# Attention's output written straight into the MLP's layout in 32-row groups, units in pairs, and keys turned by VectorE

## The chip, the cores and the metric

One Trainium2 chip, of which the kernel uses one core. The metric is the device time of one execution in microseconds (us); lower is better. "Time before" is the median of three runs.

## The reference, cut to what matters

```python
def _attn_ref(q, k, v, f_logit):                  # each (4, 8, 768, 48): batch, head, step, feature
    f = 1.0 / (1.0 + np.exp(-f_logit))
    for t in range(S):
        state = f[:, :, t, :, None] * state + np.einsum('bhd,bhe->bhde', k[:, :, t], v[:, :, t])
        y[:, :, t] = np.einsum('bhd,bhde->bhe', q[:, :, t], state)
    return y
x = _attn_ref(...).transpose(0, 2, 1, 3).reshape(3072, 384)
x = np.square(np.maximum(x @ w_in, 0)) @ w_out                         # MLP 1, 384 -> 2048 -> 384
h = x @ w_in2; return (h * np.tanh(softplus(h))) @ w_out2              # MLP 2, the same sizes
```

A recurrent attention with a forget gate for each feature, then two MLPs over the 3072 tokens.

## The kernel before, in words

**The MLPs.** Tokens are taken in 6 blocks of 512, the 2048 hidden features in 16 chunks, so an MLP has 96 *slots*. In a slot TensorE (PE) does `do_l1(i)`: nine 128x512 products into a PSUM tile `h` (L333), and `do_l2(i-2)`: nine into the three accumulators `a` (L344). Nine and not three because operands are split into a high and a low part (weights `w`, x, and gh/gl). Between the two, ScalarE (ACT) does `act_a` (relu, square, the high part gh) and VectorE (DVE) `act_b` (the low part gl, L357). The second MLP works alike with a longer activation; nothing of the change lies there.

**The attention** feeds the first MLP. The 768 steps are 12 chunks of 64, and each chunk is done for two pairs of batches: 24 *units*. Four units (two chunks) make one token block's x. A unit has y = 0 and 1 for the two batches of its pair, and does:

- `load_f`, `load_v` (SyncE's queue): the gates, keys and queries `in`, and the values `vs`;
- `v_min`, `a_exp`, `a_ln`, `v_scan`, `a_dq`, `a_dk`, `v_q`, `v_k` on DVE and ACT: the running product of gates and the scaled queries `mv` (L449) and keys (L453);
- `m_a` on PE: keys times queries (`at` L476/477, or `aq` L471 in four 64x64 quadrants of PE's array from unit 9 on); `v_mask` (L495/L498) masks it into `mv`;
- `m_t` on PE: four transposes of the keys into a PSUM tile `tr` (L486), which `a_kn` copies to `kn` by four ACT instructions (L508);
- `m_u` on PE: keys times values, the update of the state (`u` L543/544, `uq` L538 in quadrants); `v_s` (L588, L589) puts the new state beside the values of unit i+2 in `vs`;
- `m_y` on PE: y = masked products and queries times values and state. For units 0 to 7 (L518) tokens lie on the partitions, two tiles of 64 columns of the array side by side; `a_y` (ACT, L553) copies it, and `m_x` (PE, L577) transposes it into `xt`. For units 8 to 23 (L525) features lie on the partitions, 48 of 64 rows for a head; `a_y` (L558) copies it, and `y_dma` (L565 to L570) moves it by six DMAs into `ax` with the rows in the MLP's order;
- `a_x` (L602), `v_x` (L606): high and low part of x for the MLP.

**PSUM.** `h`, `at`, `aq`, `tr`, `u`, `uq`, `y` and `xt` share five banks of one pool; the accumulators have three.

**Order.** Engines run their instructions in the order of the program. Up to slot 18 this order is a list written by hand (`START`). From there `put(slot, prio, f, ...)` collects the operations of a slot and `run(i)` issues them sorted by prio; `unit(i, s)` puts those of unit i around its slot s = 4i - 17, so one unit every four slots: `m_a`, `m_t` in slot s between `do_l1` (prio 100) and `do_l2` (prio 120), `m_y`, `m_u` in slot s+2. In slots 22 to 70 the second MLP's weights are also prepared (`w2_load`, `w2_abs`, `w2_bits`, `w2_split`: L251 to L261, L306, L307).

**fp32 products in the trace.** The attention's matmuls are plain fp32, and one of them shows as two records of PE. A *round* below is the stretch in which matmuls in different tiles of the array run at once.

Of the kernel before, what the change touches and what calls it, by code (L numbers as in the profile page):

```python
# [42 lines left out]
v_k 3; v_k 2; v_q 3 1; w_low 0; m_x 0; a_x 0; m_u 0; a_kn 1; v_s 0 0; m_a 2; w_abs 1; v_x 0; load_w 3; v_mask 2 0;
m_u 1; v_s 1 0; v_s 0 1; w_shift 1; m_a 3; m_t 3; v_mask 2 1; w_hi 0; a_kn 3; m_t 2; m_warm 1; m_y 2; a_kn 2;
v_s 1 1; v_mask 3 1; v_mask 3 0; m_x 1; m_warm 1; m_y 3; m_warm 1; w_lo 0; w_top 1; load_w 4; w_abs 2; a_x 1; v_x 1;
a_y 2; w_shift 2; m_x 2; load_f 5; a_y 3; w_low 1; a_x 2; load_w 5; m_x 3; m_warm 6; load_w 6; v_end 3; a_x 3; v_x 3;
v_x 2; w_top 2; do_l1 0; w_hi 1; w_abs 3; load_v 4; w_lo 1; w_low 2; do_l1 1; w_abs 4; w_shift 3; v_min 5; w_hi 2;
load_w 7; w_top 3; a_exp 5; w_lo 2; w_shift 4; m_u 3; load_w 8; w_low 3; act_a 0; act_b 0; w_abs 5; w_top 4; w_hi 3;
w_shift 5; load_w 9; do_l1 2; act_a 1; w_lo 3; w_low 4; w_hi 4; act_b 1; load_w 11; w_top 5; w_lo 4; w_low 5;
v_s 3 0; do_l2 0; do_l1 3; do_l2 1; act_a 2; act_b 2; do_l1 4; w_abs 6; w_hi 5; w_abs 7; w_shift 6; w_lo 5; w_top 6;  # L50
do_l2 2; act_a 3; w_abs 8; w_shift 7; w_low 6; load_f 4; a_ln 5; w_hi 6; w_top 7; act_b 3; v_s 3 1; act_a 4; w_lo 6;
w_abs 9; do_l1 5; do_l2 3; w_low 7; w_hi 7; load_v 5; act_b 4; w_shift 8; load_f 7; act_a 5; w_shift 9; load_w 10;
do_l1 6; w_top 8; load_f 6; do_l2 4; v_end 2; w_lo 7; w_top 9; w_low 8; act_b 5; act_a 6; w_hi 8; w_abs 11; v_min 4;
v_scan 5; w_lo 8; load_v 7; do_l1 7; w_low 9; load_w 14; a_exp 4; do_l2 5; a_ln 4; act_b 6; a_dq 5; w_hi 9; a_dk 5;
v_q 5 1; w_abs 10; w_lo 9; v_scan 4; do_l1 8; act_a 7; do_l2 6; v_k 5; a_dq 4; v_q 5 0; act_a 8; do_l1 9; a_dk 4;
w_shift 10; act_b 7; w_top 10; v_q 4 1; m_t 5; v_min 6; w_shift 11; v_k 4; act_a 9; act_b 8; m_a 5; load_w 12;
do_l2 7; v_min 7; m_u 2; v_q 4 0; do_l2 8; w_low 10; a_kn 5; m_a 4; w_top 11; m_t 4; a_exp 7; v_mask 5 0; w_hi 10;
a_ln 7; w_lo 10; v_end 5; v_end 4; w_low 11; act_b 9; w_abs 12; w_hi 11; w_shift 12; v_mask 5 1; w_top 12; do_l1 10;
do_l2 9; w_lo 11; act_a 10; do_l1 11; w_low 12; load_w 13; w_hi 12; w_abs 13; act_b 10; do_l2 10; v_mask 4 1;
w_lo 12; v_s 2 0; v_s 2 1; do_l1 12; act_a 11; w_shift 13; v_mask 4 0; w_abs 14; a_exp 6; act_b 11; m_y 5; a_ln 6;  # L60
w_top 13; w_shift 14; a_kn 4; do_l2 11; w_low 13; v_scan 6; w_hi 13; m_y 4; w_lo 13; a_y 5; act_a 12; do_l1 13;
v_scan 7; w_top 14; a_dq 7; act_b 12; a_dk 7; load_w 15; w_low 14; v_q 7 0; m_u 5; v_s 5 0; v_k 7; a_dq 6; v_q 7 1;
# [5 lines left out]
v_s 6 1; do_l2 14; a_dk 8; a_exp 9; v_s 6 0; v_k 8; act_a 15; v_q 8 0; act_b 15; a_ln 9; do_l1 16; v_scan 9; m_t 8;
v_end 8; act_a 16; load_v 10; do_l1 17; a_dq 9; v_q 8 1; v_q 9 0; v_end 9; a_dk 9; load_v 9; do_l2 15; a_kn 8;
v_q 9 1; do_l1 18; act_b 16; m_a 8; v_mask 8 1; v_mask 8 0; do_l2 16; m_y 8; m_u 8; act_a 17; a_y 8; load_f 10;  # L70
y_dma 8; act_b 17; v_k 9; v_s 8 0; v_s 8 1
# [23 lines left out]
def stepwise_path(ctx: ExitStack, tc: tile.TileContext, qkf, vv, ws, out):  # L95
# [41 lines left out]
    with tc.For_i(0, NC, 1) as c:  # L137
        for bp in range(2):
            nc.sync.dma_start(out=fkq[:, bp].rearrange("p j h t -> p j (h t)"), in_=qkf[bass.ds(c, 1), bp][0][0:112])
            for y in range(2):  # L140
                nc.sync.dma_start(out=val[64 * y:64 * y + 64, bp],
                                  in_=vv[bass.ds(c, 1), bp, y][0].rearrange("t h e -> t (h e)"))
# [7 lines left out]
        for t in range(C):  # L150
# [12 lines left out]
            for bp in range(2):  # L163
                for k in range(3):
                    o = yp[:, k].rearrange("p (b y t) -> p b t y", b=2, y=2)[:, bp, t]
                    T.matmul(out=o[0:96], lhsT=qs[:, bp, 96 * k:96 * k + 96], rhs=pair)
                    T.matmul(out=o[96:128], lhsT=qs[:, bp, 288 + 32 * k:320 + 32 * k], rhs=pair)
# [46 lines left out]
def fast_path(ctx: ExitStack, tc: tile.TileContext, flag, qkf, vv, w1, w2, out):  # L214
# [15 lines left out]
    st_p = ctx.enter_context(tc.tile_pool(name="stg", bufs=2))  # L230
# [6 lines left out]
    late, done = [], set()  # L237
# [143 lines left out]
    def attention(at, at1):  # L381
# [10 lines left out]
        vs = [lt.tile([128, 2 * DM + 32], F32, tag=f"vs{i}", name=f"vs{i}") for i in range(4)]  # L392
# [5 lines left out]
        es = [at1.tile([112, H, C + 1], F32, name=f"es{i}") for i in range(3)]  # L398
        U = {}

        def vsv(i):
            return vs[i % 4][:, 0:2 * DM].rearrange("p (y h e) -> p y h e", y=2, h=H)
# [60 lines left out]
        def m_a(i):  # L463
            kt = head(fkq(i)[1])
            m = mv[i % 2]
            if i >= QUAD:
                a = [h_p.tile([128, 4, C], F32, tag="h", name="aq") for _ in range(2)]
                for h in range(H):
                    o = 64 * (h % 2)
                    for y, r in ((0, 64), (1, 0)):  # L470
                        T.matmul(out=a[y][o:o + 64, h // 2], lhsT=kt[r:r + 48, h], rhs=m[r:r + 48, y, h])  # L471
                U[i]["a"] = a
                return
# [4 lines left out]
            U[i]["a"] = a  # L478

# [31 lines left out]
        def m_y(i):  # L511
            m, s = mv[i % 2], vs[i % 4]
            if i < NE:
                ps = h_p.tile([128, H, D], F32, tag="h", name="y")
                for h in range(H):
                    for y, k in ((0, 112), (1, 128)):
                        c0 = y * DM + h * D
                        T.matmul(out=ps[64 * y:64 * y + 64, h], lhsT=m[0:k, y, h], rhs=s[0:k, c0:c0 + D])  # L518
            else:
                ps = h_p.tile([128, 4, 2, C], F32, tag="h", name="y")  # L520
                for y, k in ((0, 112), (1, 128)):
                    for h in range(H):
                        o = 64 * (h % 2)
                        c0 = y * DM + h * D
                        T.matmul(out=ps[o:o + 64, h // 2, y], lhsT=s[0:k, c0:c0 + 64], rhs=m[0:k, y, h])  # L525
            U[i]["y"] = ps

        def m_u(i):
# [415 lines left out]
```

## Time and profile before

| | |
|---|---|
| time, median of 3 runs (lowest, highest) | 899.26 us (898.05, 899.27) |
| the profiled execution: its time, its span | 899.2 us, 897.5 us |
| PE busy | 884.0 us, 99% |
| VectorE busy | 676.2 us, 75% |
| ScalarE busy | 618.3 us, 69% |
| PE's granted clock | 0.999 |

Busy is the time in which an engine ran an instruction; the span is from the first instruction to the last. The attention with the first MLP takes the first 495 us of the span.

### The profile page before, as it was taken

The numbers are of one execution on the slowest core, as the hardware profiler recorded it, in microseconds if no ns is written. First come the engines' busy times: TensorE is split into PE (matmuls) and PEld (weight loads), VectorE is DVE, ScalarE is ACT, GpSimd is POOL, SyncE is SP. The second block draws the span as 40 slices with busy tenths as digits, with TensorE's granted clock in tenths as the row PEclk, the third lists the DMA queues.
The fourth block names the chain that finished last, engine by engine and source line by source line (L and its number), as shares of the span: only waits on it lengthen the run. The fifth ranks groups of instructions, "written<-read, shape, count | busy, mean of one in ns | idle before, by whom it ended". The sixth has DMA issues, their size and how long they took to land.

```text
span 897.5 us, 15329 instructions
## 1 busy us (share of the span) xinstructions
PE 884.0 (99%) x5927; PEld 725.6 (81%) x5927; DVE 676.2 (75%) x1146; ACT 618.3 (69%) x1131; POOL 5.2 (1%) x21
## 2 busy tenths in 40 slices
PE   8999999999999999999999999999999999999997
PEld 7788888888787887888888888888888888888885
DVE  8999976876778877772222788888788888888785
ACT  8798776876787778764544566666666676666664
POOL 2000000000000000000000000000000000000000
PEclk9999999999999999999999999999999999999999
DMA  9922223455536454632453100200200200200001
GB/s 319 392 91 106 91 96 114 166 172 167 186 132 230 152 205 163 213 106 81 175 202 115 71 0 1 72 1 0 71 1 1 71 0 1 72 1 0 36 1 38
DMA packets 34735, 92.29 MB, mean 103 GB/s; under 512 B 5216, under 2 KB 11360, under 8 KB 34656
## 3 DMA queue, kind: packets, MB, share of 16 engines
q1 hardware_dynamic: 34656, 91.25, 29.4%
q8 instruction: 48, 0.79, 0.4%
q14 instruction: 31, 0.25, 0.1%
HBM read 66.06 MB, written 22.02 MB: 98 GB/s over the span
## 4 chain that ended last, share of the span: by engine, by line
PE 87%; ACT 4%; DVE 4%; DMA 2%; SPq 1%; issue 1%; ACTq 0%
PE h L333 41%; PE a L344 40%; PE y L525 2%; DMA ax<-ay 1%; PE tr L486 1%; PE aq L471 1%; PE y L518 1%; PE at L476 1%; ACT r L716 1%; PE uq L538 1%; DMA sr<-in_w_dram 1%; PE u L543 1%; DVE mv L449 0%; ACT r L715 0%; ACT gh L352 0%
## 5 line engine op out<-in xcount | busy, mean ns | idle before, releaser
L333 PE MATMUL h<-x,w 128*128 128x512 f32 x1728 | 425.5, 390 | 0.7 <-ACT x L602 0.4
L344 PE MATMUL a<-gh,w 128*128 128x512 f32 x1146 | 388.3, 394 | 0.0
L333 PEld LDWEIGHTS h<-x,w 128*128 128x128 f32 x1728 | 323.5, 188 | 70.4 <-DVE x L606 1.0
L344 PEld LDWEIGHTS a<-gh,w 128*128 128x128 f32 x1146 | 215.2, 188 | 46.0
L344 PE MATMUL a<-gl,w 128*128 128x512 f32 x573 | 223.6, 391 | 0.0
L782 ACT ACTIVATE e<-e 128x512 f32<-128x512 f32 x95 | 60.1, 632 | 117.5 <-DVE e L781 117.5
L344 PEld LDWEIGHTS a<-gl,w 128*128 128x128 f32 x573 | 107.7, 188 | 22.1 <-DVE gl L357 0.7
L357 DVE TENSOR_TENSOR gl<-r,gh 128x512 fp32r<-128x512 f32 x96 | 65.8, 686 | 78.8 <-ACT gh L352 76.7
L781 DVE TENSOR_SCALAR e<-h 128x512 f32<-128x512 f32 x95 | 65.7, 692 | 60.7 <-PE h L333 58.1
L715 ACT ACTIVATE r<-h 128x512 f32<-128x512 f32 x96 | 56.6, 590 | 49.0 <-PE h L333 48.6
L776 ACT ACTIVATE r<-u,cst 128x512 f32<-128x512 f32 x94 | 67.9, 723 | 8.7 <-DVE u L790 2.7
L790 DVE SCALAR_TENSOR_TENSOR u<-e 128x512 f32<-128x512 f32 x95 | 65.9, 694 | 10.0 <-ACT e L782 0.7
L357 DVE TENSOR_TENSOR gl<-g,gh 128x512 fp32r<-128x512 f32 x95 | 65.7, 692 | 0.0
L778 DVE TENSOR_TENSOR e<-h,u 128x512 f32<-128x512 f32 x94 | 64.3, 684 | 0.0
L785 DVE TENSOR_TENSOR g<-e,r 128x512 f32<-128x512 f32 x94 | 64.2, 683 | 0.0
L352 ACT ACTIVATE gh<-r 128x512 fp32r<-128x512 f32 x96 | 60.7, 633 | 3.1
L716 ACT ACTIVATE r<-r 128x512 f32<-128x512 f32 x96 | 60.7, 632 | 3.0
L352 ACT ACTIVATE gh<-g 128x512 fp32r<-128x512 f32 x95 | 60.1, 633 | 3.1 <-DVE g L809 0.8
L777 ACT ACTIVATE r<-r 128x512 f32<-128x512 f32 x94 | 59.5, 633 | 3.0
L606 DVE TENSOR_TENSOR x<-ax,x 128x384 fp32r<-128x384 f32 x16 | 8.9, 556 | 35.9 <-ACT x L602 35.9
L602 ACT ACTIVATE x<-ax 128x384 fp32r<-128x384 f32 x16 | 8.4, 525 | 38.5 <-DMA ax<-ay 38.3
L508 ACT ACTIVATE kn<-tr 64x192 f32<-64x192 f32 x88 | 28.4, 322 | 6.1 <-PE tr L486 5.2
(120 smaller groups left out, 729.2 us busy)
## 6 DMA issues: line engine op xcount, KB each, us to landing
in<-in_qkf_dram SPq DMA_DIRECT2D x18, 768.0 KB, 5.8
r<-in_w_dram SPq DMA_DIRECT2D x16, 768.0 KB, 9.6
sr<-in_w_dram SPq DMA_DIRECT2D x32, 384.0 KB, 3.5
w2d<-sw SPq DMA_DIRECT2D x32, 384.0 KB, 3.1
w<-w2d SPq DMA_DIRECT2D x32, 384.0 KB, 3.5
vs<-in_vv_dram SPq DMA_DIRECT2D x48, 96.0 KB, 5.6
x2d<-ot SPq DMA_DIRECT2D x18, 256.0 KB, 2.1
x<-x2d SPq DMA_DIRECT2D x6, 768.0 KB, 5.1
```

The costliest lines, as they stand in the source:

```text
L333: T.matmul(out=ps, lhsT=w[:, k * 128:(k + 1) * 128], rhs=x[:, s, k], start=(i == 0), stop=(i == 8))
L344: T.matmul(out=acc[m], lhsT=w[:, m * 128:(m + 1) * 128], rhs=gx, start=(fc == 0 and i == 0), stop=(fc == FC - 1 and i == 2))
L352: A.activation(out=gh, in_=g, func=AF.Copy)
L357: V.tensor_tensor(out=gl, in0=g, in1=gh.bitcast(F32), op=ALU.subtract)
L716: A.activation(out=r, in_=r, func=AF.Square)
L776: A.activation(out=r, in_=u, func=AF.Ln, bias=two)
L777: A.activation(out=r, in_=r, func=AF.Exp, scale=-1.0)
L778: V.tensor_tensor(out=e, in0=hp, in1=u, op=ALU.mult)
L781: V.tensor_scalar(out=e2, in0=ps, scalar1=20.0, scalar2=None, op0=ALU.min)
L782: A.activation(out=e2, in_=e2, func=AF.Exp)
L785: V.tensor_tensor(out=g, in0=e, in1=r, op=ALU.mult)
L790: V.scalar_tensor_tensor(out=u2, in0=e2, scalar=2.0, in1=e2, op0=ALU.add, op1=ALU.mult)
```

## The change

`m_y` no longer writes y to be moved, but x itself, features on the partitions: 32 matmuls for a unit, each into 32 rows of the array's output at column position 0, 32, 64 or 96. Where a group of 32 rows spans two heads, two matmuls accumulate into it, each with zero columns where the other has its head. For that `vs` holds 64 columns for a head (`HC`), values are loaded with 16 zero columns (128 KB instead of 96), and the host rotates the columns of the odd heads and permutes the weights' rows to match. `a_y`, `m_x` and `y_dma` are gone, and `a_x`, `v_x` read the PSUM tile.

Units 10 to 23 are done in pairs every eight slots: at slot s = 8(i//2) - 15 the `uq` of the pair before and the `aq` of this pair, at s+4 both y. Units 9 to 21 have their keys turned by VectorE (`v_turn`, one instruction) and copied by eight ACT instructions (`a_turn`) instead of four PE transposes and four copies. The entries of `START` for the removed operations are gone, a few later ones with them change place; `EARLY` (a few weight loads of the second MLP) and the scope of the pool `stg` change too.

```diff
@@ def attention
+        def quarters_a(*units):
+            both = [h_p.tile([128, 2, 4, C], F32, tag="h", name="aq") for _ in range(2)]
+            for i in units:
+                U[i]["a"] = a = [t[:, i % 2] for t in both]
+                kt, m = head(fkq(i)[1]), mv[i % 2]
+                for h in range(H):
+                    o = 64 * (h % 2)
+                    for y, r in ((0, 64), (1, 0)):
+                        T.matmul(out=a[y][o:o + 64, h // 2], lhsT=kt[r:r + 48, h], rhs=m[r:r + 48, y, h])
...
+        def v_turn(i):
+            V.transpose(out=kts[i % 2], in_=inp[i % 2][:, 1])
+
+        def a_turn(i):
+            t = kts[i % 2].rearrange("p (h b t) -> p h b t", h=H, b=2)
+            for y in range(2):
+                for d, n in ((0, 32), (32, D - 32)):
+                    for b in range(2):
+                        r, o = 64 - 64 * y + d, 64 * y + 32 * b
+                        A.activation(out=kns[i % 2][o:o + 32, y, :, d:d + n], in_=t[r:r + 32, :, b, 0:n], func=AF.Copy)
...
         def m_y(i):
...
+            x = h_p.tile([128, 3, 2, C], F32, tag="h", name="y")
+            groups = [[] for _ in range(4)]
+            for a in range(H // 2):
+                for j, parts in enumerate((((0, 0),), ((0, 32), (1, 48)), ((1, 80),))):
+                    k, g = divmod(3 * a + j, 4)
+                    groups[g] += [(k, g, 2 * a + b, 2 * HC * a + col, n == 0, n + 1 == len(parts))
+                                  for n, (b, col) in enumerate(parts)]
+            for y, rows in ((0, 112), (1, 128)):
+                for four in zip(*groups):
+                    for k, g, h, col, first, final in four:
+                        T.matmul(out=x[32 * g:32 * g + 32, k, y], lhsT=s[0:rows, y, col:col + 32], rhs=m[0:rows, y, h],
+                                 start=first, stop=final)
+            U[i]["x"] = x.rearrange("p k y t -> p k (y t)")
...
-        def a_y(i):
...
-        def y_dma(i):
...
-        def m_x(i):
...
             else:
-                put(s + 3, 12, y_dma, i)
-            put(s + 3, 22, v_s, i, 0)
-            put(s + 3, 22, v_s, i, 1)
-            put(s + 4, 16, a_x, i)
-            put(s + 4, 30, v_x, i)
+                odd = i % 2
+                s += 1 - odd
+                end = s + 4
+                if i + 2 < NU:
+                    put(s - 1, 27, v_turn, i)
+                    put(s + 1 + odd, 14, a_turn, i)
+                    put(s + 9, 12 - odd, v_s, i, 0)
+                    put(s + 10, 9 - odd, v_s, i, 1)
+                if odd:
+                    if i - 2 >= PAIRS:
+                        put(s, 110, quarters_u, i - 3, i - 2)
+                    put(s, 111, quarters_a, i - 1, i)
+                put(s + 2, 11 - odd, v_mask, i, 0)
+                put(s + 3, 11 - odd, v_mask, i, 1)
+            put(end, 110, m_y, i)
+            put(end + 1, 12, a_x, i)
+            put(end + 1, 13, v_x, i)
```

PE's order around one unit of before (unit 13, slots 35 to 37). `mv_155` and `in_145` are the odd units' buffers, `a_1648` the first accumulator:

```order
L333 MATMUL h<-x,w_1073 128x512 x9
L471 MATMUL aq<-mv_155,in_145 64x64 x16
L486 MATMUL tr<-idn,in_145 128x112 x4
L344 MATMUL a_1648<-gh,w_902 128x512
...
L333 MATMUL h<-x,w_1192 128x512 x9
L525 MATMUL y<-mv_155,vs_153 64x64 x16
L538 MATMUL uq<-vs_153,kn_157 48x48 x16
L344 MATMUL a_1648<-gh,w_1073 128x512
```

And around one pair of the change, first its `m_y` (units 10 and 11, slot 29), then the place where the next pair begins (slot 33):

```order
L330 MATMUL h<-x,w_1246 128x512 x9
L545 MATMUL y<-mv_154,vs_152 32x64 x32
L545 MATMUL y<-mv_155,vs_153 32x64 x32
L341 MATMUL a_1722<-gh,w_1111 128x512
...
L330 MATMUL h<-x,w_651 128x512 x9
L489 MATMUL uq<-vs_152,kn_156 48x48 x16
L489 MATMUL uq<-vs_153,kn_157 48x48 x16
L478 MATMUL aq<-mv_154,in_144 64x64 x16
L478 MATMUL aq<-mv_155,in_145 64x64 x16
L341 MATMUL a_1722<-gh,w_1530 128x512
```

Two places in eight slots now hold what four held; `tr` is gone, and y is 32 smaller matmuls for a unit instead of 16.

ScalarE's order behind such a place, of before (one unit) and of the change (a pair; `kt_164` and `kt_165` are the turned keys):

```order
L352 ACTIVATE gh<-r 128x512
L508 ACTIVATE kn_157<-tr 64x4x48 x4
L426 ACTIVATE es_162<-in_144 112x8x64
```

```order
L349 ACTIVATE gh<-r 128x512
L500 ACTIVATE kn_156<-kt_164 32x8x32 x2
L500 ACTIVATE kn_156<-kt_164 32x8x16 x2
L500 ACTIVATE kn_156<-kt_164 32x8x32 x2
L500 ACTIVATE kn_156<-kt_164 32x8x16 x2
L248 ACTIVATE wbit,wsum<-sr 128x384 x2
L721 ACTIVATE r<-h 128x512
L722 ACTIVATE r<-r 128x512
L349 ACTIVATE gh<-r 128x512
L500 ACTIVATE kn_157<-kt_165 32x8x32 x2
```

Four copies from PSUM became eight narrower ones from SBUF for a unit, two units close behind each other.

VectorE's order ahead of a unit's `aq`, of before (the state `v_s` of the unit before it stands ahead of its queries, L449, and keys, L453):

```order
L357 TENSOR_TENSOR gl<-r,gh 128x512
L588 TENSOR_TENSOR vs_151<-uq,vs_153 48x4x48 x2
L589 TENSOR_TENSOR vs_151<-vs_151,f 48x384
L588 TENSOR_TENSOR vs_151<-uq,vs_153 48x4x48 x2
L589 TENSOR_TENSOR vs_151<-vs_151,f 48x384
L449 TENSOR_TENSOR mv_154<-in_144,eq 48x512 x2
L453 TENSOR_TENSOR in_144<-in_144,es_161 112x512
```

and ahead of a pair's in the change:

```order
L447 TENSOR_TENSOR mv_155<-in_145,eq 48x512 x2
L451 TENSOR_TENSOR in_145<-in_145,es_161 112x512
L492 STREAM_TRANSPOSE kt_164<-in_144 128x512
L492 STREAM_TRANSPOSE kt_165<-in_145 128x512
L354 TENSOR_TENSOR gl<-r,gh 128x512
L304 SCALAR_TENSOR_TENSOR sw<-wbit,sw 128x384 x2
L354 TENSOR_TENSOR gl<-r,gh 128x512
L567 TENSOR_TENSOR vs_153<-uq,vs_151 48x4x48 x2
L568 TENSOR_TENSOR vs_153<-vs_153,f 48x8x48
```

The state now comes after the pair's products (`uq` is at the pair's own place), and the turning stands between the keys and the next `gl`.

## Rows read from the trace of the kernel before

**Rows 1.** The page: engines' busy us (share of the span).

```profile
PE 884.0 (99%) x5927; PEld 725.6 (81%) x5927; DVE 676.2 (75%) x1146; ACT 618.3 (69%) x1131; POOL 5.2 (1%) x21
```

**Rows 2.** Windows; columns: span, busy PE, PEld, DVE, ACT, POOL, clock, DMA share, GB/s.

```profile
153.01:172.40 19.39, 19.39 (x174) 15.74 (x173) 14.77 (x32) 15.09 (x34) 0.00 (x0) 1.00 0.51 181
231.68:388.44 156.76, 156.00 (x1376) 125.75 (x1377) 125.00 (x246) 118.06 (x250) 0.00 (x0) 1.00 0.52 177
14.00:34.45 20.45, 17.97 (x349) 15.89 (x345) 20.10 (x32) 16.35 (x44) 0.00 (x0) 1.00 1.02 387
104.81:117.45 12.64, 12.61 (x174) 10.38 (x172) 12.38 (x20) 10.79 (x26) 0.00 (x0) 1.00 0.49 162
```

**Rows 3.** Timeline of PE, one unit's four slots; columns: start, length, instruction.

```profile
153.01 0.69 PE L471 MATMUL aq<-mv,in 48*64 48x64 f32 x32
153.63 0.60 PE L486 MATMUL tr<-idn,in 112*128 112x112 f32 x4
154.01 0.49 PE L344 MATMUL a<-gh,w 128*128 128x512 f32 x1
...
156.18 2.21 PE L333 MATMUL h<-x,w 128*128 128x512 f32 x9
...
160.27 2.20 PE L333 MATMUL h<-x,w 128*128 128x512 f32 x9
162.40 1.15 PE L525 MATMUL y<-mv,vs 112*64 112x64 f32 x32
163.48 0.57 PE L538 MATMUL uq<-vs,kn 64*48 64x48 f32 x32
163.99 0.50 PE L344 MATMUL a<-gh,w 128*128 128x512 f32 x1
```

**Rows 4.** Timeline of PE, two products of one output row, second MLP.

```profile
664.80 0.19 PE L766 MATMUL nover<-fmin,cst 112*1 112x8 f32 x2
664.85 0.25 PE L767 MATMUL nover<-wsum,cst 128*1 128x48 f32 x2
```

**Rows 5.** Timeline, where PE idled in 134 to 400 us; [idle before <- releaser].

```profile
231.68 0.69 PE L471 MATMUL aq<-mv,in 48*64 48x64 f32 x32 [1.01 <-PE h L333]
...
271.02 0.69 PE L471 MATMUL aq<-mv,in 48*64 48x64 f32 x31 [0.30 <-issue]
...
352.29 0.49 PE L333 MATMUL h<-x,w 128*128 128x512 f32 x1 [0.36 <-ACT x L602]
...
351.72 0.52 ACT L602 ACTIVATE x<-ax 128x384 fp32r<-128x384 f32 x1 [3.70 <-DMA ax<-ay]
```

**Rows 6.** Timeline of DVE ahead of the first of these.

```profile
226.94 0.73 DVE L588 TENSOR_TENSOR vs<-uq,vs 48x192 f32<-48x192 f32 x2
...
230.90 0.68 DVE L453 TENSOR_TENSOR in<-in,es 112x512 f32<-112x512 f32 x1
```

**Rows 7.** Timeline of PE, end of the start, and among units 4 to 7.

```profile
34.51 0.74 PE L333 MATMUL h<-x,w 128*128 128x512 f32 x2 [0.27 <-DVE x L606]
...
106.52 0.87 PE L577 MATMUL xt<-idn,ay 128*128 128x128 f32 x6
```

**Rows 8.** Groups by form, 134 to 400 us; busy, mean ns | idle before.

```profile
L508 ACT ACTIVATE kn<-tr 64x192 f32<-64x192 f32 x52 | 16.7, 322 | 0.5
L558 ACT ACTIVATE ay<-y 112x512 f32<-112x512 f32 x14 | 8.1, 581 | 0.0
...
L434 DVE TENSOR_TENSOR_SCAN es<-es,cap 112x520 f32<-112x520 f32 x14 | 17.3, 1237 | 2.8 <-ACT es L430 2.8
L453 DVE TENSOR_TENSOR in<-in,es 112x512 f32<-112x512 f32 x14 | 9.5, 678 | 0.0
L423 DVE TENSOR_SCALAR in<-in 112x512 f32<-112x512 f32 x13 | 5.4, 414 | 0.0
```

**Rows 9.** View of one line, L820 and L553: durations ns lowest/median/highest.

```profile
L820 ACT ACTIVATE e<-e x2: 402/402/403, 885.2 to 885.5; 128x256 f32<-128x256 f32 x2
...
L553 ACT ACTIVATE ay<-y x16: 239/337/435, 18.9 to 109.1; 128x288 f32<-128x288 f32 x8, 128x96 f32<-128x96 f32 x8
```

More of the change, by code (lines that the diff above doesn't have):

```diff
@@ L43 @@
[L43 to L47, printed above, removed]
@@ L58 @@
[L58 to L62, printed above, removed]
@@ L68 @@
[L68 to L71, printed above, removed]
+load_v 0; load_w 0; a_ln 2; a_exp 3; eye_kn 0; load_v 1; load_f 2; m_t 0; m_warm 2; v_end 1; v_k 1; v_q 1 1; load_v 2;
@@ L165, in stepwise_path @@
                     o = yp[:, k].rearrange("p (b y t) -> p b t y", b=2, y=2)[:, bp, t]
[L166 to L167 removed]
+                    T.matmul(out=o, lhsT=qs[:, bp, 128 * k:128 * k + 128], rhs=pair)
         A.activation(out=x, in_=yp[:, 0:3], func=AF.Copy)
@@ L390, in head @@
             return t.rearrange("p (h t) -> p h t", h=H)
-        vs = [lt.tile([128, 2 * DM + 32], F32, tag=f"vs{i}", name=f"vs{i}") for i in range(4)]
+        vs = [lt.tile([128, 2, H, HC], F32, tag=f"vs{i}", name=f"vs{i}") for i in range(4)]
         mv = [lt.tile([128, 2, H, C], F32, tag=f"mv{i}", name=f"mv{i}") for i in range(2)]
@@ L398, in attention @@
         es = [at1.tile([112, H, C + 1], F32, name=f"es{i}") for i in range(3)]
+        kts = [at1.tile([128, 512], F32, name=f"kt{i}") for i in range(2)]
         U = {}
         def vsv(i):
-            return vs[i % 4][:, 0:2 * DM].rearrange("p (y h e) -> p y h e", y=2, h=H)
+            return vs[i % 4][:, :, :, 0:D]
         def load_in(i, j, k):
@@ L465, in m_a @@
             m = mv[i % 2]
[L466 to L473, printed above, removed]
             a = h_p.tile([128, H, C], F32, tag="h", name="at")
@@ L478, in m_a, with quarters_u @@
             U[i]["a"] = a
+        def quarters_a(*units):
[7 more added lines that the diff above has]
+                        T.matmul(out=a[y][o:o + 64, h // 2], lhsT=kt[r:r + 48, h], rhs=m[r:r + 48, y, h])
+        def quarters_u(*units):
+            both = [h_p.tile([128, 2, 4, D], F32, tag="h", name="uq") for _ in range(2)]
+            for i in units:
+                U[i]["u"] = u = [t[:, i % 2] for t in both]
+                sv, kn = vsv(i), kns[i % 2]
+                for h in range(H):
+                    o = 64 * (h % 2)
+                    for y in range(2):
+                        k = slice(64 * y, 64 * y + 64)
+                        T.matmul(out=u[y][o:o + 48, h // 2], lhsT=kn[k, y, h], rhs=sv[k, y, h])
+        def v_turn(i):
+            V.transpose(out=kts[i % 2], in_=inp[i % 2][:, 1])
+        def a_turn(i):
+            t = kts[i % 2].rearrange("p (h b t) -> p h b t", h=H, b=2)
+            for y in range(2):
+                for d, n in ((0, 32), (32, D - 32)):
+                    for b in range(2):
+                        r, o = 64 - 64 * y + d, 64 * y + 32 * b
+                        A.activation(out=kns[i % 2][o:o + 32, y, :, d:d + n], in_=t[r:r + 32, :, b, 0:n], func=AF.Copy)
         def m_t(i):
@@ L511, in m_y @@
         def m_y(i):
[L512 to L526, printed above, removed]
+            m, s = mv[i % 2], vs[i % 4].rearrange("p y h c -> p y (h c)")
+            x = h_p.tile([128, 3, 2, C], F32, tag="h", name="y")
[11 more added lines that the diff above has]
+            U[i]["x"] = x.rearrange("p k y t -> p k (y t)")
         def m_u(i):
@@ L905, in _layout @@
     qkf[:, :, 0:48] = a[:, :, 1]
-    vv = v.reshape(2, 2, H, NC, C, D).transpose(3, 0, 1, 4, 2, 5)
-    row = np.arange(384).reshape(8, 48)
-    perm = []
-    tail = np.concatenate([row[6], row[7]])
-    for i in range(3):
-        perm += [row[2 * i], row[2 * i + 1], tail[32 * i:32 * i + 32]]
-    perm = np.concatenate(perm)
+    turned = np.concatenate([np.arange(32, D), np.arange(32)])
+    v = v.copy()
+    v[:, 1::2] = v[:, 1::2][..., turned]
+    vv = np.zeros((NC, 2, 2, C, H, HC), v.dtype)
+    vv[..., 0:D] = v.reshape(2, 2, H, NC, C, D).transpose(3, 0, 1, 4, 2, 5)
+    perm = np.arange(DM).reshape(H, D)
+    perm[1::2] = perm[1::2][:, turned]
+    perm = perm.reshape(DM)
     def wl(a, b):
```

155 lines of the change are left out of this document (73 added, 82 removed).

## The prediction, made before the run

> **What bounds the kernel now.** I read the page first: PE is busy 99% of the span, VectorE 75%, ScalarE 69% [rows 1]. Nothing here is worth anything unless it takes time off PE's own queue, or a wait of PE. So the second question is what one unit of the attention costs PE. The windows give 19.39 us for the four slots of one unit, with PE busy throughout [rows 2]. The timeline beneath shows the slots: an `h` block and an `a` block with nothing between take 160.27 - 156.18 = 4.09 us, four slots 16.36, so a unit costs 19.39 - 16.36 = **3.03 us**. Its blocks, from start to next start [rows 3]: `aq` 0.62, `tr` 0.38, `y` 1.08, `uq` 0.51, together 2.59. The other 0.44 is what the `h` ahead and the `a` behind run longer, 0.22 for each of the two places where small matmuls cut in.
>
> How small matmuls are paid is read from the same rows. `aq` is 32 records in four quadrants, 8 rounds, in 0.62; `y` is 32 records in two 64-column tiles, 16 rounds, in 1.08. Eight rounds more cost 0.46, so a round takes 57.5 ns and a block 0.16 to begin with. `uq` (8 rounds, 48 columns in and out) gives (0.51 - 0.16)/8 = 44 ns.
>
> Then what stood in PE's way: in 134 to 400 us three waits of 1.01, 0.30 and 0.36 us, 1.67 in all [rows 5]. The first is an `aq` behind VectorE: the unit's keys (L453) are ready only at 231.58, and `v_s` of the unit before stands in VectorE's queue ahead of them [rows 6]. The third is an `h` behind ScalarE's x, which sat 3.70 us waiting for the six DMAs.
>
> **The change, part by part.** All sums are against the profiled execution, 899.2 us; the median of the runs shown is 0.06 above it.
>
> *The new y.* 32 matmuls for a unit are 64 records in four column tiles: 16 rounds of four where 16 rounds of two were. No row shows four tiles of 128 rows at once; `aq` shows four at once as quadrants. If all four run together, what is the round? `y` of before has 57.5 ns with 64 columns out and 64 streamed. From below: two records of 8 columns take 0.19, two of 48 columns 0.25 [rows 4], 0.75 ns a column, 48 ns for 64. I take 55, nearer to the row that is most alike. A unit's y is then 16 x 0.055 + 0.16 = 1.04, practically what it was. The saving is not in y itself but in what follows it.
>
> *Pairs, and no `tr`.* The place at the start of a pair holds `uq` for two units, 16 rounds of 44 ns: 0.86; `aq` for two, 16 rounds of 57.5: 1.08; and 0.22 around: 2.16. The first of seven such places has no `uq`: 1.30. The place of y holds 32 rounds: 1.76 + 0.16 + 0.22 = 2.14. Units 10 to 23 after: 6 x 2.16 + 1.30 + 7 x 2.14 = 29.24. Before: 12 units at 3.03 and the last two, which have neither `tr` nor `uq`, at 3.03 - 0.38 - 0.51 = 2.14: 40.64. **-11.4 us.** Of that `tr` is 12 x 0.38 = 4.6; the rest is half of the cuts into the MLP's stream and of the 0.16s. Unit 9 is not paired but loses its `tr`: **-0.4**.
>
> *Units 0 to 7: no `xt`.* For units 0 to 3 that is hidden: from 14.00 to 34.45 VectorE is busy 20.10 of 20.45 us [rows 2], and the first `h` products wait for its x, idling to 34.51 [rows 7]. None of VectorE's work there goes, so 0. For units 4 to 7 twelve transposes leave, six of which took 0.87 [rows 7]: 1.7 at most. But in those 12.64 us VectorE is busy 12.38 [rows 2], and the `u` products and the next block's x wait for its queue, so 0 at least. I take the middle: **-0.8**.
>
> *ScalarE.* `a_turn` is eight copies. Four have 256 elements a partition, as L820 has: 402 ns. Four have 128, between the 96 of L553's shorter form (239) and the 192 of L508 (322): some 275 [rows 8, 9]. That is 2.71 us, against four L508 (1.29) and one L558 (0.58) that go: +0.84 a unit.
>
> *VectorE.* No row has a turning. The nearest in size is L453 (112x512 elements, 0.68); between the cheapest and the dearest instruction on such a tile, L423 (0.41) and L434 (1.24) [rows 8], I take 0.68 a unit. The Trainium skill ("VectorE: DVE Perf Modes", The three transpose paths) has 311 ns for a 128x128 bf16 tile, so four of these would be estimated at 1.24 us, and no run here shows it; by it the sum would be the same as long as the work is hidden.
>
> Is it hidden? In 231.68 to 388.44 (156.76 us, eight units) VectorE was busy 125.00 and ScalarE 118.06 [rows 2]. Eight units less 0.88 each (3.03 - 2.15), less the 1.67 of waits, is some 148 us. VectorE gets 125.00 + 8 x 0.68 = 130.4, or 88%; with the bounds 128.3 to 134.9, 87 to 91%. ScalarE gets 118.06 + 8 x 0.84 = 124.8, 84%. Both stay below PE, so on average it costs nothing; in the slots where a pair's work is bunched it may.
>
> *The waits.* Behind a pair's place, four of five PSUM banks hold `uq`, `uq`, `aq`, `aq`. The next `h` needs the fifth, which ScalarE's relu of the last `h` frees; between lie the place (1.9) and an `a` block (2.2), 4 us of cover for an instruction that takes 0.6. The `h` after that needs `v_s` of y = 0 of both units, some 8 us after the place begins; VectorE has 4 x 0.36 + 2 x 0.55 = 2.5 us to do for it and a `gl` ahead. y waits for `v_mask` four slots after the place, 16 us. What goes: the first wait, since `v_s` no longer stands ahead of the pair's keys in VectorE's order, and the third with the six DMAs (96 issues in all leave SyncE's queue; the loads of values grow by a third, and are issued two slots or more ahead). So -1.67. What comes: I put 0.1 us on each of seven pairs, which is what 14 units had on average (1.67/14 = 0.12): +0.7. Net **-1.0**.
>
> Sum: 899.2 - 11.4 - 0.4 - 0.8 - 1.0 = **885.6 us**. Own range 883.5 to 888.5: the round between 48 and 57.5 over seven pairs (-1.6 to +0.6), `xt` (+-0.8), waits (-0.7 to +2).
>
> **The rivals.**
>
> *A: the four column tiles don't run four at once.* Each holds all 128 rows, so four moving operands would have to enter the same rows at a time; before, no more than two do, in y as in the quadrants. If they go two and two, a unit has 32 rounds, y costs 32 x 0.0575 + 0.16 = 2.00 instead of 1.04, and units 4 to 23 pay 20 x 0.96 = 19.2: 904.8 us, **slower**. The same comes out if a record must follow the one before in y's 0.92/32 = 29 ns. It decides from a round of four at 55 + 13.6/(20 x 16) = 97 ns on. For it: nothing shows four. Against it: `aq`'s 32 records pass in 0.46 us, 14 ns each, so neither issue nor weight loads hold a record for 29 ns, and y's round did not care that its two tiles share all their rows. The Trainium skill ("TensorEngine Tiling (Array Packing)", Instruction Overhead) speaks for it: a matmul has some 60 cycles of overhead whatever its columns, and tiling should not be taken from a dimension that is already small. By that 64 records, estimated at 25 ns, would be 1.6 us a unit and the time about 900; `aq`'s 14 ns a record disagree. Chance 0.11.
>
> *B: bunching.* ScalarE has two `a_turn` (5.4 us) in two slots of 4.1, besides its relu, square, copy and the weights; VectorE has `v_s` and `v_mask` of two units (4.2 us) at the same place. An `h` that waits for a bank, or an `aq` for keys, at each pair: 1.01 is the size that such a wait had before. Seven of them instead of 0.7 make 885.6 + 6.4 = 892.0; at 2 us each it is 899, and the gain is gone. For it: 88% on average is more in the heavy slots. Against it: the cover counted above. Chance 0.16.
>
> *C: y is quicker.* `uq` with 48 columns had 44 ns where 64 had 57.5, 0.9 ns a column of output. If the round followed the output columns alone, 32 would give 29 ns: y 0.62, units 8 to 23 16 x 0.42 = 6.7 less: 878.9. Against it: the 64 streamed columns of rows 4, which alone want 48. Chance 0.07.
>
> *D: it does nothing,* the time at 897 to 901, because some wait not seen takes all of it: 0.02.
>
> **How the numbers follow.** The forecast has 0.64, and that is 885.6. The range: A (0.11) and the end of B above 894 (0.03) stay out above; below, 879.5 takes in the slow half of C. A measurement of this kernel tells about 0.2%, 1.8 us: faster is the forecast, C, and nearly all of B, 0.86; slower is A, 0.11; the same 0.03.
>
> **What would show it.** PE, in a pair's eight slots of 32.7 us: two places of about 2.2 us, 37.0 us from one pair to the next against 38.8 for two units. The y block, 128 records in 1.9 to 2.0 us; 3.8 would be A, 1.1 C. Waits of PE ahead of `h` two slots after a pair's `aq`, with VectorE's `v_s` or ScalarE as releaser, would be B. The `aq` should wait for no keys any more, and no `h` for x. VectorE at 88%, ScalarE at 84% between 230 and 380 us; a turning much above 1.24 us, or copies of 32 partitions much above 0.4, would move these. The prediction is wrong if the round is, or if one wait returns at every pair.

## The result

The changed kernel takes **891.05 us** (median of four, 889.39 to 892.60) against 898.94 (898.05 to 899.27): ratio 0.9913, 95% interval 0.9894 to 0.9933. It is 7.9 us faster; 13.6 were forecast. The profiled execution is the slowest of the four (892.60, span 890.8), so 1.5 us of what follows is its own.

The page of the changed kernel, busy us (share), as [rows 1]:

```profile
PE 872.1 (98%) x6619; PEld 720.4 (81%) x6619; DVE 683.9 (77%) x1159; ACT 626.6 (70%) x1151; POOL 6.5 (1%) x21
```

Its windows, cut at the first `h`, at the `h` of slot 16, at that of slot 80 (units 8 to 23 lie between these two), at the end; and a piece of the start. Columns as in [rows 2]:

```profile
0.00:38.24 38.24, 32.35 (x570) 29.90 (x571) 30.66 (x56) 24.01 (x52) 6.53 (x21) 0.87 0.96 300
38.24:121.47 83.23, 81.97 (x874) 65.77 (x873) 82.10 (x118) 68.97 (x131) 0.00 (x0) 1.00 0.43 145
121.47:421.06 299.59, 295.74 (x3132) 242.41 (x3131) 231.88 (x455) 237.10 (x500) 0.00 (x0) 1.00 0.46 155
421.06:890.80 469.74, 462.04 (x2048) 382.31 (x2046) 339.24 (x532) 296.51 (x471) 0.00 (x0) 1.00 0.13 44
24.00:36.00 12.00, 10.19 (x198) 9.11 (x202) 9.68 (x15) 5.68 (x14) 0.00 (x0) 0.57 1.03 399
```

The same cuts lie at 33.76, 117.45 and 427.35 us before. So the start lost 4.5 us (38.24 - 33.76), slots 0 to 15 gained 0.5 (83.23 against 83.69), the pairs' stretch gained 10.3 (299.59 against 309.90), and the rest 0.4 (469.74 against 470.15): within it the second MLP's blocks are 1.4 us shorter, and 1.0 us is lost behind them, where the last results are written out. Sum -6.7, the difference of the spans (897.5, 890.8).

The timeline of PE at a pair's two places, which answers to [rows 3]:

```profile
237.92 2.20 PE L330 MATMUL h<-x,w 128*128 128x512 f32 x9
240.05 0.94 PE L489 MATMUL uq<-vs,kn 64*48 64x48 f32 x64
240.81 1.15 PE L478 MATMUL aq<-mv,in 48*64 48x64 f32 x64
241.89 0.50 PE L341 MATMUL a<-gh,w 128*128 128x512 f32 x1
...
258.43 2.00 PE L545 MATMUL y<-mv,vs 112*32 112x64 f32 x128
260.36 0.50 PE L341 MATMUL a<-gh,w 128*128 128x512 f32 x1
```

From start to next start: `uq` 0.76 (0.86 forecast), `aq` 1.08 (1.08), y 1.93 for two units (1.92). Four column tiles do run at once. From this pair to the next 36.86 us (37.0).

The groups by form that answer to [rows 8, 9], 134 to 400 us:

```profile
L492 DVE STREAM_TRANSPOSE kt<-in 128x512 f32<-128x512 f32 x13 | 8.4, 679 | 0.0
L500 ACT ACTIVATE kn<-kt 32x256 f32<-32x256 f32 x52 | 21.6, 415 | 0.8
L500 ACT ACTIVATE kn<-kt 32x128 f32<-32x128 f32 x52 | 16.0, 308 | 0.6
```

The turning takes 0.679 us (0.68 taken), the copies 0.415 and 0.308 (0.402 and 0.275).

And the waits that answer to [rows 5]. PE behind the pair's place at slot 65, and ScalarE there:

```profile
353.91 0.50 PE L341 MATMUL a<-gh,w 128*128 128x512 f32 x1
...
357.43 0.73 PE L330 MATMUL h<-x,w 128*128 128x512 f32 x2 [1.17 <-ACT r L721]
```

```profile
354.91 0.60 ACT L363 ACTIVATE ot<-a 128x512 f32<-128x512 f32 x1 [3.78 <-PE a L341]
356.29 0.60 ACT L363 ACTIVATE ot<-a 128x512 f32<-128x512 f32 x1 [0.79 <-PE a L341]
356.79 0.59 ACT L721 ACTIVATE r<-h 128x512 f32<-128x512 f32 x1
```

The waits of before are gone, but at slots 33, 49 and 65 (206.39, 282.25 and 357.43 us) an `h` waits 1.17 us for ScalarE's relu. ScalarE had been idle for 3.78 us. It stood at the copies of a token block's accumulators, which are complete only as the `a` block runs to its end; the relu of an `h` long finished, whose PSUM bank PE needs, stands behind.

### The profile page after: what moved, and what is told of

Its sections match the earlier page's. It is cut to its first block, busy times and chain, and to the rows that moved or that the text cites. A ratio compares the mean times of both kernels' runs of the same rounds, so it can differ in the third digit from the quotient of the medians.

```text
span 890.8 us, 16582 instructions
## 1 busy us (share of the span) xinstructions
PE 872.1 (98%) x6619; PEld 720.4 (81%) x6619; DVE 683.9 (77%) x1159; ACT 626.6 (70%) x1151; POOL 6.5 (1%) x21
## 4 chain that ended last, share of the span: by engine, by line
PE 83%; DVE 9%; DMA 4%; ACT 2%; issue 1%; SPq 1%; ACTq 0%
PE a L341 40%; PE h L330 40%; DMA r<-in_w_dram 2%; PE y L545 2%; DVE wbit L255 1%; DMA vs<-in_vv_dram 1%; DVE w L280 1%; DVE gl L354 1%; DVE wbit L258 1%; PE aq L478 1%; PE uq L489 1%; DVE vs L571 1%; DVE mv L520 1%; DVE wbit L252 1%; DVE mv L447 0%
## 5 line engine op out<-in xcount | busy, mean ns | idle before, releaser
L721 ACT ACTIVATE r<-h 128x512 f32<-128x512 f32 x96 | 56.5, 588 | 52.8 <-PE h L330 52.1
L500 ACT ACTIVATE kn<-kt 32x256 f32<-32x256 f32 (+1 forms) x104 | 37.6, 362 | 1.4
L432 DVE TENSOR_TENSOR_SCAN es<-es,cap 112x520 f32<-112x520 f32 x24 | 29.6, 1232 | 0.8 <-ACT es L428 0.8
L447 DVE TENSOR_TENSOR mv<-in,eq 48x512 f32<-48x512 f32 x40 | 27.4, 685 | 1.4 <-ACT eq L437 0.6
```

## The experiments

Times are medians with their own runs of before; the "stretch" is that from the `h` of slot 16 to that of slot 80 in the profiled execution.

### The copies of the accumulators behind the relu

```diff
-            if s == FC - 1:
-                evac(accs.pop(b), lambda m: x2d[b][:, m])
+            if s == FC - 1 and 0 < b < 5:
+                put(i + 3, 6, evac_b, b)
+            elif s == FC - 1:
+                evac_b(b)
...
+        def evac_b(b):
+            evac(accs.pop(b), lambda m: x2d[b][:, m])
```

> The changed kernel, with the three copies of a finished token block's accumulators (ot<-a, blocks 1 to 4) issued behind the next slot's relu, square and high part instead of ahead of them. Theory: the three waits of 1.17 us ahead of an h behind the pairs' places at slots 33, 49 and 65 come from ScalarE's order, in which the relu that frees the fifth PSUM bank stands behind copies that wait for the accumulators: the waits go, 3.5 us less than the changed kernel, some 887.5 us. Rival: the bank is held by uq until VectorE's state update in any case, and the wait only changes its releaser: 890 to 891 us, with waits of 0.5 to 1.2 us left at these places.

886.92 us, ratio 0.9874 (0.9858 to 0.9891), 4.1 less than the change by the medians, 3.5 by the ratios. Windows of the start, of slots 0 to 15 and of the stretch, then ScalarE's timeline at slot 33:

```profile
0.00:35.22 35.22, 28.18 (x571) 25.79 (x571) 30.50 (x56) 24.00 (x51) 6.51 (x21) 1.00 0.95 317
35.22:118.50 83.28, 81.93 (x874) 65.74 (x873) 82.15 (x118) 68.98 (x131) 0.00 (x0) 1.00 0.43 149
118.50:414.34 295.84, 295.19 (x3132) 242.34 (x3131) 231.79 (x455) 237.50 (x500) 0.00 (x0) 1.00 0.46 157
```

```profile
198.11 0.60 ACT L726 ACTIVATE r<-h 128x512 f32<-128x512 f32 x1 [2.15 <-PE h L330]
198.74 0.63 ACT L727 ACTIVATE r<-r 128x512 f32<-128x512 f32 x1
199.41 0.63 ACT L349 ACTIVATE gh<-r 128x512 fp32r<-128x512 f32 x1
200.81 0.60 ACT L363 ACTIVATE ot<-a 128x512 f32<-128x512 f32 x1 [0.78 <-PE a L341]
```

The relu now runs as soon as its `h` is there, the three waits are gone, and the stretch is 3.75 us shorter: the theory holds. What PE still idles in the stretch is one wait of 0.65 us for a `gl`, at 361.14 us. Its start differs by 3 us though the list `START` is the same: the start varies from one profiled execution to another.

### The new y, the turning and the pairs apart

`PAIRS = 24` takes the pairs away; for y alone the turning gives way to TensorE's transposes.

```diff
-PAIRS = 10
+PAIRS = 24
...
-                    put(s, 27, v_turn, i)
...
-                    put(s + 1, 14, a_turn, i)
-                    put(s + 2, 111, quarters_u, i)
+                    if i + 2 < NU:
+                        put(s, 111, m_t, i)
+                        put(s + 1, 14, a_kn, i)
+                        put(s + 2, 111, quarters_u, i)
```

> The changed kernel with only its new y: no pairs (one unit every four slots, as before) and the keys of all units transposed by TensorE and copied from PSUM, as before. From the first h of slot 16 to that of slot 80, in which units 8 to 23 lie, the kernel before takes 309.9 us, the changed one 299.6, the one with late copies of the accumulators 295.8. Theory: the new y costs TensorE what the old one did (1.04 against 1.08 us), so this stretch takes 308 to 309.5 us (0.04 for each of 14 units, and the waits of before, 1.67 us at most), and with the later start and the second MLP's 1.4 us the time is 898 to 900 us. Rival: what left with the old y (its copy, its six DMAs) is worth more than the waits shown: 305 us or less, 895 us.

> The changed kernel without pairs: the new y, and keys turned by VectorE and copied by ScalarE, one unit every four slots. Theory: against the new y alone it saves TensorE's four transposes, 0.38 us for each of 13 units, 4.9 us: the stretch from slot 16 to 80 takes 303.5 to 305 us, the time is 893 to 895 us, so that the pairs are worth 3 to 4 us as they stand and 7 without their three waits. Rival: VectorE and ScalarE can't hide the turning (0.68 and 1.6 us more for a unit) when it comes right ahead of the unit's aq: waits of TensorE at each unit, the stretch no shorter than with the new y alone.

Both theories missed: 907.49 (ratio 1.0095, 1.0078 to 1.0112) and 910.22 us (1.0130, 1.0114 to 1.0147), slower than before, the stretch 316.28 and 320.42 us. The timelines of y alone behind slot 33 show why, ScalarE, VectorE and PE:

```profile
206.95 0.60 ACT L363 ACTIVATE ot<-a 128x512 f32<-128x512 f32 x1 [0.79 <-PE a L341]
...
209.27 0.47 ACT L581 ACTIVATE x<-y 128x384 fp32r<-128x384 f32 x1
...
209.78 0.56 DVE L585 TENSOR_TENSOR x<-y,x 128x384 fp32r<-128x384 f32 x1 [1.84 <-ACT x L581]
...
214.31 0.68 DVE L451 TENSOR_TENSOR in<-in,es 112x512 f32<-112x512 f32 x1
...
215.09 1.02 PE L478 MATMUL aq<-mv,in 48*64 48x64 f32 x32 [2.05 <-issue]
```

The copies of the accumulators hold up ScalarE's x, VectorE's x (now at prio 13, ahead of the state, queries and keys) waits for it, and the keys end 0.1 us before the `aq` starts, which stood 2.05 us. Two more `aq` wait as long (296.07 and 377.11 us), and behind the first two of the three PE's granted clock is 0.50, half of full speed, for 3.4 us each (from 215.28 and 297.20 us). So these two measure an order made for pairs, not the parts. Both again, with late copies of the accumulators and `put(end + 1, 30, v_x, i)`; what each of the two does alone was not tried:

> The new y without pairs and with TensorE's transposes, as y_alone, but with the two things put right that y_alone waited for: the accumulators' copies issued behind the next relu, and v_x back behind the state update and the queries in VectorE's order (prio 30 instead of 13). Theory: the new y itself is worth nothing or a few tenths: the stretch from slot 16 to 80 takes 308 to 309.5 us against 309.9 of before (316.3 in y_alone), time 898 to 900 us with the later start and the second MLP's 1.4 us. Rival: holding y's PSUM bank until VectorE has read it, instead of one copy of ScalarE, keeps banks short without pairs: waits ahead of aq remain, 312 us or more.

> As y_alone2, with the keys turned by VectorE and copied by ScalarE instead. Theory: TensorE's transposes are worth 0.38 us for each of 13 units: the stretch 4 to 5 us shorter than y_alone2's, 303.5 to 305 us, time 893.5 to 895 us; the remaining 8 to 9 us down to 295.8 are the pairs'. Rival: the turning stands between a unit's keys and its aq in VectorE's order, and its 0.68 us and ScalarE's 1.6 us more come back as waits at each unit: no shorter than y_alone2.

897.41 us (ratio 0.9988, 0.9978 to 0.9997) and 894.07 (0.9944, 0.9927 to 0.9961). The windows of their stretches:

```profile
119.80:426.23 306.43, 306.43 (x3185) 248.21 (x3183) 224.61 (x442) 218.45 (x448) 0.00 (x0) 1.00 0.45 151
```

```profile
120.11:422.90 302.79, 301.81 (x3132) 243.50 (x3131) 231.94 (x455) 237.41 (x500) 0.00 (x0) 1.00 0.46 153
```

Each step in the stretch: before 309.90; the new y 306.43, 3.5 less, of which 1.8 are the waits of before, and more than the 0.4 to 1.9 expected (a unit's y takes 1.03 us instead of 1.08, 0.8 for sixteen; where the other 0.9 come from stays open); the turning 302.79, another 3.6 (4.6 without a wait of 1.0 at one `aq`); the pairs 295.84, another 7.0 (8 to 9 expected). In the order as it was changed, three waits give 3.75 back.

### VectorE's room: every turning twice

```diff
-            V.transpose(out=kts[i % 2], in_=inp[i % 2][:, 1])
+            for _ in range(2):
+                V.transpose(out=kts[i % 2], in_=inp[i % 2][:, 1])
```

> The changed kernel with late copies of the accumulators (886.9 us), and each turning of keys on VectorE done twice: 13 times 0.68 us more work for VectorE, whose share goes from some 88 to 92% in that part. Theory: VectorE's work is hidden behind TensorE's, so the time stays within 1 us of 886.9 and the stretch from slot 16 to 80 within 0.7 us of 295.8. Rival: VectorE is at its limit where a pair's work is bunched, and the doubled work shows in full, 8.8 us, or at each pair by 0.7 us, 4.2 us: 891 to 896 us.

890.45 us (ratio 0.9905, 0.9888 to 0.9921), 3.5 more than with single ones by the medians, the stretch 300.30. PE's timeline behind a pair's place, and VectorE's there:

```profile
238.44 0.49 PE L341 MATMUL a<-gh,w 128*128 128x512 f32 x1
240.30 0.50 PE L341 MATMUL a<-gl,w 128*128 128x512 f32 x1 [1.37 <-DVE gl L354]
```

```profile
236.88 2.79 DVE L493 STREAM_TRANSPOSE kt<-in 128x512 f32<-128x512 f32 x4
239.59 0.65 DVE L354 TENSOR_TENSOR gl<-r,gh 128x512 fp32r<-128x512 f32 x1
```

Neither in full (8.8) nor hidden: at this pair the doubled turnings, 2.8 us in a row, stand ahead of the next `gl`, and PE waits 1.37 us for it. PE waits for a `gl` twice more. At 310.12 us, 1.45, no turning stands just ahead. At the pair before it ScalarE waited 3.81 us for VectorE's work on the weights behind the turnings (2.07 with single ones); it then worked on without a gap, waited 0.72 and 0.26 us for loads, and so its x, VectorE's keys and the `gl` behind them came late, seven slots on. The third, 0.65 at 366.68, is there with single turnings too. The timeline shows no wait for the other four pairs' turnings. So single turnings are hidden with VectorE at 89% (133.06 of 150 us in 230 to 380, with late copies), but two of six pairs have less than 1.4 us to spare.

### The start

Six runs change the start; the first two are the kernel before with wider values.

```diff
+HC = 56
...
-        vs = [lt.tile([128, 2 * DM + 32], F32, tag=f"vs{i}", name=f"vs{i}") for i in range(4)]
+        vs = [lt.tile([128, 2 * H * HC + 8], F32, tag=f"vs{i}", name=f"vs{i}") for i in range(4)]
```

> The kernel before, with 56 columns for a head in the values instead of 48, 8 of them zero: loads of 112 KB instead of 96 (the change has 128), nothing else. Theory: the first h comes later in the change because the wider loads of values hold up the first weights on the DMA engines; with half of the increase the first h comes 0.7 to 2 us later than the 33.8 us of before, and the time is 900 to 901 us. Rival: the wider loads cost nothing, and the later start is the change's removed work or its clock: first h within 0.3 us of 33.8, time 899. The slots of the second MLP that ran 0.12 us longer in before than in the change (1.4 us in all) stay if the tile's width has nothing to do with them.

> The kernel before with 56 columns for a head in the values, as in before_wide_v, but with 24 columns more of padding, so that the tile is 3712 bytes a partition (29 times 128) instead of 3616: before_wide_v ran every block of the MLPs at 2.09 us instead of 2.04, 13 us in all, and 3616 is no multiple of 64. Theory: the blocks' 0.05 us were an effect of where the tiles behind this one lie in SBUF: with 3712 the blocks take 2.04 again, and what is left is the start, with the first h 0.7 to 1.1 us later than in before (34.64 in before_wide_v): 899 to 900.5 us. Rival: the wider values themselves slow the blocks: 912 us again.

The first: 912.46 us (1.0158, 1.0141 to 1.0175), every block of the MLPs 2.09 us instead of 2.04, which neither theory had. The second, with `+ 32` for `+ 8`: blocks of 2.04 again, 899.17 us (1.0008, 0.9996 to 1.0020), the first `h` at 34.95 us, 1.2 later than before (34.64 in the first of the two). That is from one execution, itself 1.65 us above its kernel's median; by the medians the second is 0.6 slower, within the noise. Windows from 5 to 20 us of the kernel before, of the second, and of the changed one:

```profile
5.00:20.00 15.00, 14.19 (x209) 13.30 (x209) 14.24 (x20) 14.00 (x31) 1.40 (x5) 1.00 1.03 347
```

```profile
5.00:20.00 15.00, 14.31 (x206) 13.42 (x205) 13.84 (x19) 12.67 (x27) 2.61 (x10) 1.00 1.02 260
```

```profile
5.00:20.00 15.00, 14.09 (x223) 13.15 (x226) 13.04 (x18) 11.64 (x25) 2.62 (x8) 1.00 1.01 270
```

The DMA engines are busy all the time in all three (1.03, 1.02, 1.01), but they move 260 and 270 GB/s with wider values, against 347 before. All the kernels here with wider values and the same order of loads move 260 to 299 in this window, and the three below that take weights ahead of values 309 to 333. So in this window the wider values go with less throughput, and not only more bytes; why the packets take longer stays open.

The other two are the changed kernel:

```diff
-a_x 0; m_u 0; a_kn 1; ... v_mask 2 0; m_u 1;
+a_x 0; m_u 0; m_warm 8; a_kn 1; ... v_mask 2 0; m_warm 3; m_u 1;
```

> The changed kernel with eleven more warm-up matmuls in the start, eight behind the first u and three behind the third at, where TensorE idles 1.9 and 1 us. Theory: TensorE's clock was granted at half from 25 to 35 us because it had idled before, and that lengthened the start by some 2 us: with them the granted clock stays at full, the first h comes at 36 us instead of 38.2, time some 889 us. Rival: the half clock delays nothing that ends last: first h at 38, time 891 as before.

```diff
-load_v 0; load_w 0; ... load_v 2; ... load_v 3; ... load_w 1; ... load_w 2;
+load_w 0; load_v 0; ... load_w 1; load_v 2; ... load_w 2; load_v 3;
```

> The changed kernel with the loads of the first three weight chunks each issued ahead of a load of values that stood ahead of them. Theory: ScalarE waits 2.9 us for the first weights because of the wider values, and everything behind it in its queue is late, so that TensorE idles and falls to half clock; with the weights ahead the wait is under 1 us, the first h comes at 34 to 36 us, time 887 to 889 us. Rival: the values then come late, and the first y wait for them by as much: first h at 38, time 891.

892.81 us (0.9939, 0.9922 to 0.9956) and 891.36 (0.9918, 0.9901 to 0.9934): both theories missed and neither helps, first `h` at 37.87 and 36.43. With the warm-ups PE's clock falls all the same, to 0.50 from 27.72 to 31.13 us. Two more start from late copies of the accumulators:

```diff
-load_v 0; load_w 0; ... m_u 0; a_kn 1;
+load_w 0; load_v 0; ... m_u 0; m_warm 6; a_kn 1;
```

> The changed kernel with late copies of the accumulators (886.9 us), and in the start the first chunk of weights loaded ahead of the first values, and six more warm-up matmuls where TensorE waited for the third unit's keys. Theory: ScalarE's wait for the first weights (2.7 us) goes, TensorE doesn't idle long enough to fall to half clock, the first h comes at 34 to 35.5 us in the profiled execution, and the time is 1 to 2 us less, 885 to 886 us, with less spread. Rival: the start is bound by the bytes that must land in its first 20 us whatever their order, and only another load is late: 886.5 to 887.5 us.

```diff
-... load_v 2; ... load_v 3; ... load_w 1; ... load_w 2;
+... load_w 1; ... load_w 2; load_v 2; load_v 3;
```

> The changed kernel with late copies of the accumulators (886.9 us), and in the start the values of units 2 and 3 (four loads of 128 KB, used by y at some 30 us) issued behind the second and third chunk of weights instead of ahead of them, that is at some 15 to 18 us instead of 9 to 16. Theory: the wider values, read at a low rate just when early keys, queries and the first weights must land, are what makes the start longer: without these four in the way ScalarE's second weights and VectorE's keys of units 2 and 3 come in time, TensorE's wait of 1.6 us ahead of at goes, the first h comes at 33.8 to 34.6 us instead of 35.2 to 38.2, the clock stays at full, and the time is 1 to 2 us less, 885 to 886 us. Rival: the bytes that must land before the first h are the same in any order; then the first weights or y wait instead: 886.5 to 888 us.

888.91 (0.9887, 0.9865 to 0.9908) and 888.69 us (0.9894, 0.9877 to 0.9910), against 886.92: both theories missed, no better, the intervals meet. In `best1` the first `h` comes at 34.67, the earliest with the new y, but PE idles 1.83 us within a `y` at 111.10, with no releaser shown. The last one tells most. Its timeline of PE:

```profile
22.43 0.27 PE L466 MATMUL at<-mv,early 48*64 48x64 f32 x1 [0.56 <-DVE early L451]
...
26.55 0.36 PE L467 MATMUL at<-mv,early 48*64 48x64 f32 x1 [3.09 <-issue]
```

With these values out of the way the keys of unit 2 come as early as in before, where this `at` starts at 22.50. But in the middle of it PE idles 3.09 us for nothing that the profile shows, and its granted clock is 0.50 from 24.83 to 38.49 us; its first `h` is at 39.48. The changed kernel:

```profile
24.54 0.27 PE L466 MATMUL at<-mv,early 48*64 48x64 f32 x1 [1.93 <-DVE early L451]
27.00 0.37 PE L467 MATMUL at<-mv,early 48*64 48x64 f32 x1 [0.95 <-issue]
```

It idles at the same instruction, and so do all eleven kernels here that have the new y, for 0.64 to 3.09 us; in before PE runs through here, and with wider values and the old y (the second of the two kernels) it idles 0.23. The trace's packets of the instruction queue point to the cause: a 16 KB packet ends at 25.51, 24.39, 25.22, 24.69, 23.69 and 25.15 us in the changed kernel, with late copies, `warm`, `loads_first`, `best1` and `values_late`, and PE goes on 1.28 to 1.49 us after it each time; in the other five it is 1.29 to 1.39 us, and `best1`'s idle time at 111.10 ends 1.38 us after such a packet. The new y has twice as many matmuls for a unit, each with its weight load. That PE waits there for its instructions is inferred from these times; no run took it away.

The clock is the third part. From that instruction to the first `h` the changed kernel takes 11.24 us, at a granted 0.57 over 24 to 36 us; with late copies, at 1.00 throughout, 9.55. That is 1.7 us for the same work. The other kernels bear it out: the four with the new y that keep full clock take 9.55 to 9.63 us; those at half for 4.4, 5.5, 6.8, 8.0, 8.1 and 11.9 us of this piece take 10.30, 10.46, 10.71, 11.19, 11.24 and 12.93 (`warm`, with more matmuls in it, left out). In the changed kernel the clock fell at 24.86 us, behind an idle time of 1.93 us; with late copies PE had idled 1.64 and 1.25 us, in `unpaired` 2.29, and both kept their clock, so the runs don't say what decides.

## Why the prediction came out as it did

The time fell on the side that was forecast, with more than half of the size: 891.05 us lies above the forecast's own range (883.5 to 888.5) and inside the wide one (879.5 to 894). That it lies near rival B's 892.0 is chance, since the start took most of the difference and B doesn't speak of it.

The step at which the sum was off by most is "For units 0 to 3 that is hidden ... None of VectorE's work there goes, so 0". Whether the removed work was hidden there no run shows; that nothing else changes in the start is wrong. The prediction counted the wider loads only in the steady state ("issued two slots or more ahead"). In the start the DMA engines are always busy, and with half of the increase the first `h` came 0.9 and 1.2 us later in the two executions profiled. With PE's wait inside `at` and, in some executions, half the clock, it came 1.5 to 4.5 us later with the changed list.

The second is in "The waits": "4 us of cover for an instruction that takes 0.6". The cover is there, but the relu could not use it: the accumulators' copies stand ahead of it in ScalarE's order once in 16 slots, where a token block of the MLP ends, and at 33, 49 and 65 this falls on a pair's place, where four of the five banks are held. "What comes" measured 3.85 us against 0.7. It is rival B in size at three of seven pairs, but an order, not bunching; with the turnings doubled, VectorE's bunched work came out as waits of 1.37 and 1.45 us behind two of six pairs.

The rest stood. Without the idle time of PE (1.78 before, 3.85 after) the stretch went from 308.12 to 295.74, 12.4 us; forecast were 11.4 and 0.4. y was forecast at 1.04 us and took 1.03 for one unit, so rivals A and C fell: 128 records in 1.93 us less 0.16 are 14 ns each. The Trainium skill's 60 cycles of overhead a matmul ("TensorEngine Tiling (Array Packing)", Instruction Overhead), 25 ns as estimated, do not add up over tiles that run together: 14 ns a record decide against it here. The time by that estimate, which the prediction puts at about 900, is some 897 by its own terms (0.56 us more for each of 20 units). The turning's 0.68 from the nearest row was right (0.679). The estimate of 1.24 us from the Trainium skill ("VectorE: DVE Perf Modes", The three transpose paths) was not. VectorE and ScalarE, forecast at 88 and 84% between 230 and 380 us, were both busy 86% (129.50 and 128.69 of 150 us). Slots 0 to 15 gained 0.5 instead of 0.8. Not foreseen: the second MLP's blocks are 1.4 us shorter. In before two `h` and two `a` blocks of each token block take 2.09 and 2.11 us instead of 2.04; with wider values alone (the second of the two kernels) they still do, so it is not that tile's width at 3712 bytes. What else of the change does it (the weights' early loads, the place of a pool) was not tried.

So of 13.6 us forecast some 3 went to three waits and 4.5 in this execution to the start (1.5 to 3.0 in the profiled executions of the other kernels that have this list); 1.4 came from elsewhere, of which the end took 1.0 back. The first is got back by moving the accumulators' copies of four token blocks: 886.92 us, the fastest kernel here, 1.3 above the forecast.

## What to carry to other kernels

When banks are short, look at what stands ahead of the instruction that frees one in its own engine's order, not only at how long it takes: an idle engine can be stuck at a copy whose source isn't finished. Cost a stretch in which the DMA engines are busy all the time apart from the steady state: here it held 1.5 to 4.5 us that no term of the sum had. And an edit taken out of the order made for it (the unpaired runs) measures that order, not the edit.

## What the runs showed of the hardware that was not expected

- Four tiles of 3616 bytes a partition instead of 3712 (3200 in before) among the kernel's tiles made every block of nine 128x512 products take 2.09 us instead of 2.04, 13 us in all. Where the tiles behind them lie is what differs; 3616 is 56.5 times 64, 3712 is 58 times, 3200 is 50 times. That this is the reason was not tried with other sizes.
- Four 32-column tiles with all 128 rows run together at 14 ns a record of 64 columns, as two tiles of 64 columns ran at 29.
- PE idled 0.64 to 3.09 us within a series of small matmuls in the start of eleven kernels, and went on 1.28 to 1.49 us after the end of an instruction packet of 16 KB each time.
